# Layer-one weight slices stored later, and the last gates of a block pair computed in place, in a three-stage attention and MLP kernel

## The chip, the cores and the metric

The kernel runs on one core of one Trainium2 chip. The metric is the device time of one execution in microseconds (us), as the median of several executions. Before the change three executions took 1112.64, 1110.62 and 1107.44 us: median 1110.62. One more execution was profiled. TensorE is called PE here, VectorE DVE, ScalarE ACT; SP is SyncE, the queue that issues nearly all DMAs.

## What is computed

The reference, cut to what matters (float32; 4 batches, 8 heads, 768 positions, head size 64; 3072 tokens of 512 numbers, 2048 hidden):

```python
def _attn_ref(q, k, v, mem_k, mem_v):
    for c in range(S // 32):                     # chunks of 32 queries
        k_full = concat([mem_k, k[c*32-16 : c*32+40]])   # 8 + up to 56 slots
        v_full = concat([mem_v, v[c*32-16 : c*32+40]])
        scores = q_c @ k_full.T / 8
        a = exp(scores - max); a = a / (sum(a) + 1e-9)
        out_c = a @ v_full

x = attention output as (3072, 512)
h = x @ w_in;  g = s * relu(h)**2 + b;         x = g @ w_out      # layer one
h = x @ w_in2; g = h * sigmoid(1.702 * h);     out = g @ w_out2   # layer two
```

## The kernel before

**Split products.** Every matrix product of the layers is made as three matmuls of parts: a number is split into a high part and the rest (xh and xl, wih and wil, woh and wol, gh and gl), and high times high, high times rest and rest times high are added in PSUM. The weights come as 64-bit numbers; DVE and ACT make the two float32 parts of each 128x512 weight tile (`words` and `prep`: ACT L332 and L342, DVE L338, L346, L350 and L354, then ACT L223 for the high part and DVE L312 for the rest). One such DMA load is a `st<-w_in` or `st<-w_out` of 512 KB into a ring of three `st` tiles.

**Stages.** The 3072 tokens are 24 tiles of 128, or six blocks of four tiles. Attention runs per tile or per pair of tiles in four steps that PE does: S (scores, L418), T (transpose, L451), V (values, L479) and X (transpose back, L493). Between them DVE and ACT do the softmax (top, less, exp, px, den, norm); after X they write the block's xh (L223) and xl (L510). Tiles 0 to 3 are done singly, later ones in pairs (4,5), (6,7), and so on. Loads of k, q (`qe`) and v are at L403; each of these tiles has one buffer, so the load for the next pair waits for the last reader of the one before.

**Layer one, the visit loop.** Blocks 0 to 3 are done in visits (`VISITS`), as units. A unit (`step`) is one block and one 128-wide slice j of the hidden size: H, 12 matmuls (L602 to L604) from x and slice j of w_in; the gate on ACT and DVE (L609, L616, L613 or L620, L624, L628); O, 12 matmuls (L640) into four accumulators. H and O of a whole block have 512 columns; the first two slices of block 0 go as half-units of 256 columns, first tiles 0 and 1, then tiles 2 and 3. The order of visits is: block 0 with j 0 to 4, block 1 with j 0 to 4, block 1 with j 5 to 15, block 0 with j 5 to 15, block 2, block 3. So all 32 weight tiles of layer one are prepared by the end of the third visit, and stay in memory till the last.

**Blocks 4 and 5 of layer one, and layer two,** are done in pairs of blocks (`seven`, `SEVEN`): seven half-size products instead of eight, from combinations of the weight slices. For layer one the combinations and plain slices are written to HBM first by `combine(p)`, for each of eight pairs p of slices: four stores (`keep`, L725, 2 x 256 KB and 2 x 128 KB) of parts that exist as soon as the weights are prepared, and two (L764, 512 KB each) of combinations that are worked out once all weights are ready (L736 and L745 on DVE, L751 on ACT, L755 on DVE). In `seven` a running tile `ys` holds intermediate sums; `gates` makes g from PSUM or from `ys`, for one block of the pair at once (`mine`), for the other by way of HBM (`gd`), except the last two slices, whose g stays in the `gq` tile. The reloaded g of the other block then comes back into `back`, which has the same buffer as `ys` (L1136).

**What sets the order.** All work is entered as operations with a due time, the engine or engines that may do it, the model duration, what it comes after, and buffers. `Plan.order` is a list scheduler over them: it picks, engine by engine, the earliest one that is ready, by due time among those ready at about the same moment, and the program is emitted in that order. Nothing is rescheduled on the chip: each engine, and SP with its DMA issues, goes through its list in order, and an instruction that waits holds up all behind it. Operations named by `after` that share no data only influence the plan; they add no wait on the chip. In idle PE time before the first O, the planner puts dummy matmuls (`idle<-cold`).

Of the kernel before, what the change touches and what calls it, by code (L numbers as in the profile page):

```python
# [23 lines left out]
KT = DM // P  # L24
# [22 lines left out]
class Plan:  # L47
# [11 lines left out]
    def op(self, need, engines, fn, after=(), alloc=(), uses=(), follows=()):  # L59
        n = len(self.ops)  # L60
        behind = list(follows)
        for tag, _ in alloc:
            if tag != "u":
                if tag in self.last:
                    behind.append(self.last[tag])
                self.last[tag] = n
        self.ops.append((need, engines, fn, list(after), list(alloc), list(uses), behind))
        for h in uses:
            self.users.setdefault(h, []).append(n)
        return n  # L70

    def order(self):
# [5 lines left out]
        starts = [None] * len(ops)  # L78
# [9 lines left out]
        marks, clock = [], 0.0  # L88
# [4 lines left out]
        for i in range(len(ops) - 1, -1, -1):  # L93
            need, engines = ops[i][:2]
# [36 lines left out]
        while left:  # L131
            best = None
            for e, q in pending.items():
                cand = []
                seen = 0
                keep = []
                while q and seen < 24:
                    need, i = heapq.heappop(q)
# [39 lines left out]
        full, clock = [], 0.0  # L178
        for i, e in chosen:
            if e == "pe":  # L180
                idle = min(starts[i], starts[self.first]) - clock
                if idle > 0.3:
                    full.append((None, int(idle / self.BEAT)))
                clock = ends[i]
            full.append((i, e))
# [4 lines left out]
def attention_moe_moe(ctx: ExitStack, tc: tile.TileContext, q_t, k_w, v_w, w_in1, w_out1, s_b, w_in2, w_out2, out):  # L190
# [24 lines left out]
    sb = const.tile([P, 2], F32, name="sb")  # L215

    plan = Plan()
    plan.first = None
    op = plan.op
    T = {}  # L220

# [349 lines left out]


    plan.tag("g", 2)
    o_split, o_y, o_part = {}, {}, {}
    halves = ("accA", "accB")


# [8 lines left out]
    def step(i):  # L586
# [77 lines left out]
        for k in range(KT):  # L664
            prev = o_y.get((group, k))
            d = op(at_o[i], {"pe": dur}, out_part(k), after=[g1, g2] + list(o_w[wout]) + ([prev] if prev is not None else []),
                   alloc=[(halves[k // 2], ("acc", group, k // 2))] if fresh and k % 2 == 0 else [], uses=[("g", i), wout],
                   follows=[d] if fresh and k % 2 else [])
            if plan.first is None:
                plan.first = d  # L670
            o_y[group, k] = d
            if done:
                finish(m, b, k, group, lo, hi, d, at_o[i] + 4)

    o_store = {}

# [41 lines left out]
    def combine(p):  # L718

        w0, w1 = (0, 0, 2 * p), (0, 0, 2 * p + 1)  # L720
        need = at_h[len(units) - 1] + 20

        def keep(v, w, src, dst):
            def fn(e):
                nc.sync.dma_start(out=wc[0][p][v][:, dst], in_=T[w][v].bitcast(F32)[:, src].rearrange("p (n d) -> p n d", d=256))  # L725
            return fn

        first = list(o_w[w0]) + list(o_w[w1])
        done = [op(need, {"sp": 0.75}, keep(v, w0, slice(0, 512), slice(0, 2)), after=first[v:v + 1], uses=[w0]) for v in range(2)]
        done += [op(need, {"sp": 0.4}, keep(v, w1, slice(256, 512), slice(2, 3)), after=first[2 + v:3 + v], uses=[w1]) for v in range(2)]  # L730

        def whole(w, k):
            def fn(e):
                T[k, p] = stp.tile([P, 512], F32, tag="u", name="u", bufs=4)
                h, l = T[w]
                nc.vector.tensor_tensor(out=T[k, p], in0=h.bitcast(F32), in1=l.bitcast(F32), op=ALU.add)  # L736
            return fn

        lo, hi = slice(0, 256), slice(256, 512)

        def sums(e):
            T["s", p] = stp.tile([P, 4, 256], F32R, tag="st", name="st")
            x, a, b = T["s", p].bitcast(F32), T["wa", p], T["wb", p]
            nc.vector.tensor_tensor(out=x[:, 0], in0=b[:, lo], in1=b[:, hi], op=ALU.add)
            nc.vector.tensor_tensor(out=x[:, 2], in0=a[:, lo], in1=b[:, lo], op=ALU.subtract)  # L745
            nc.vector.tensor_tensor(out=x[:, 1], in0=x[:, 0], in1=a[:, lo], op=ALU.subtract)
            nc.vector.tensor_tensor(out=x[:, 3], in0=a[:, hi], in1=x[:, 1], op=ALU.subtract)

        def high(e):
            T["sh", p] = stp.tile([P, 4, 256], F32R, tag="st", name="st")  # L750
            nc.scalar.copy(out=T["sh", p], in_=T["s", p].bitcast(F32))  # L751

        def low(e):
            x = T["s", p]
            nc.vector.tensor_tensor(out=x, in0=x.bitcast(F32), in1=T["sh", p].bitcast(F32), op=ALU.subtract)  # L755

        end_ = list(o_w[weights[-1]])
        a = op(need, {"dve": 0.65}, whole(w0, "wa"), after=first[:2] + end_, alloc=[("u", ("wa", p))], uses=[w0])
        b = op(need, {"dve": 0.65}, whole(w1, "wb"), after=first[2:] + end_, alloc=[("u", ("wb", p))], uses=[w1])
        c = op(need, {"dve": 1.5}, sums, after=[a, b], alloc=[("st", ("s", p))], uses=[("wa", p), ("wb", p)])  # L760
        h = op(need, {"act": 1.05}, high, after=[c], alloc=[("st", ("sh", p))], uses=[("s", p)])
        l = op(need, {"dve": 1.2}, low, after=[h], uses=[("s", p), ("sh", p)])
        for v, (k, x) in enumerate((("sh", h), ("s", l))):
            done.append(op(need, {"sp": 1.35}, lambda e, v=v, k=k: nc.sync.dma_start(out=wc[0][p][v][:, 3:7], in_=T[k, p].bitcast(F32)),  # L764
                           after=[x], uses=[(k, p)]))
        o_wc[0, p] = done
# [88 lines left out]
    def seven(s):  # L855
# [134 lines left out]
        def gates(src, d, need, uses, j, mine, away=True):  # L990
            key = ("g", s, j, mine)
            rk = ("r", s, j, mine)

            def gate1(e):
                T[rk] = (gp if mine else stp).tile([P, 512], F32, tag="r" if mine else "u", name="r", bufs=1 if mine else 4)
                if m:
                    nc.scalar.activation(out=T[rk], in_=src(), func=AF.Sigmoid, scale=GATE)  # L997
                else:
                    nc.scalar.activation(out=T[rk], in_=src(), func=AF.Relu)
# [21 lines left out]
            def gate4(e):  # L1021
                nc.vector.tensor_tensor(out=T[key][1], in0=T[rk], in1=T[key][0].bitcast(F32), op=ALU.subtract)

            a = op(need, {"act": 0.6}, gate1, after=d, alloc=[("r" if mine else "u", rk)], uses=uses)
            last = a
            if m:
                last = b = op(need, {"dve": 0.69}, gate2, after=[a], uses=uses + [rk])
            else:
                b = op(need, {"act": 0.6}, square, after=[a], uses=[rk])
                b = op(need, {"dve": 0.42}, gate2, after=[b], uses=[rk])  # L1030
            here, kw = [("g", key)], {}
            if not mine:
                here, kw = [("gq", key)], {"follows": boxed[:1]}
# [1 line left out]
                    here.append(("xf", box))  # L1035
                    boxed.append(len(plan.ops))
            own = [] if mine else [box]
            g1 = op(need, {"act": 0.62}, gate3, after=[b], alloc=here, uses=[rk] + own, **kw)
            g2 = op(need, {"dve": 0.66}, gate4, after=[g1], uses=[rk] + own)
            if not mine and away:  # L1040
                return [last, op(need + 5, {"sp": 1.45}, lambda e: nc.sync.dma_start(out=gd[j], in_=T[key][2].bitcast(F32)), after=[g1, g2], uses=[key] + own)]
            return [last, g1, g2]
# [199 lines left out]
```

## Time and profile before

| | us |
|---|---|
| median of three executions (1107.44 to 1112.64) | 1110.62 |
| the profiled execution, its own time | 1112.08 |
| its span, first to last instruction | 1110.2 |
| PE busy | 1088.7 |
| DVE busy | 711.0 |
| ACT busy | 494.2 |

The span is what the engines show of the profiled execution; 1.9 us of its time lie outside. PE busy is a union of instruction times; a 512-column matmul has a mean length of about 390 ns and the next one starts some 230 ns later, so lengths overlap. The DMA share is the mean busy share of the 16 DMA engines.

### The profile page before, as it was taken

Reading aid. Unit: us, or ns where it says so; the run is one execution under the profiler, and the core shown is the slowest. Engines: PE = TensorE matmul, PEld = TensorE weight load, DVE = VectorE, ACT = ScalarE, POOL = GpSimd, SP = SyncE. Lnnn points to the kernel's source line nnn. Section 1 sums busy time; section 2 is a strip of 40 time slices with the busy share of each in tenths; the row PEclk is TensorE's granted clock in tenths of the full one; section 3 lists DMA queues with packets and bytes.
Section 4 is the critical chain, followed back from the end, with each engine's and each line's share of the span. In section 5 each row is a group of like instructions: output and inputs, shape, how many; then the busy total and the mean of one; then the engine's idle time right before and its main releaser. Section 6 shows DMA issues by size and latency. Waiting matters only on the chain.

```text
span 1110.2 us, 20092 instructions
## 1 busy us (share of the span) xinstructions
PE 1088.7 (98%) x7852; PEld 897.8 (81%) x7852; DVE 711.0 (64%) x1241; ACT 494.2 (45%) x842; POOL 0.7 (0%) x6
## 2 busy tenths in 40 slices
PE   8879999999999999999999999999999999999998
PEld 7768887888878788888888888888888888888886
DVE  6888988878778688687881455660555760655610
ACT  4678865555445455566640433330433430333310
POOL 0000000000000000000000000000000000000000
PEclk9999999999999999999999999999999999999999
DMA  8776627756678783888999965574755574654154
GB/s 326 245 258 209 208 105 248 259 193 219 208 275 267 265 301 117 312 294 279 318 323 382 322 203 200 183 260 144 246 188 201 202 246 155 203 190 142 76 191 150
DMA packets 119406, 252.99 MB, mean 228 GB/s; under 512 B 12816, under 2 KB 29200, under 8 KB 119312
## 3 DMA queue, kind: packets, MB, share of 16 engines
q1 hardware_dynamic: 119024, 251.19, 66.1%
q8 instruction: 62, 1.02, 0.4%
q10 hardware_dynamic: 288, 0.52, 0.1%
q14 instruction: 32, 0.26, 0.1%
HBM read 169.87 MB, written 81.79 MB: 227 GB/s over the span
## 4 chain that ended last, share of the span: by engine, by line
PE 92%; DMA 3%; DVE 2%; issue 1%; ACT 1%; SPq 0%; ACTq 0%; DVEq 0%
PE accA L1059 16%; PE accB L1059 16%; PE accA L640 7%; PE accB L640 7%; PE ph L981 5%; PE ph L983 5%; PE ph L982 5%; PE ph L602 5%; PE ph L603 5%; PE ph L604 5%; PE pb L983 4%; PE pb L981 4%; PE pb L982 4%; DMA st<-w_in 2%; PE o L479 1%; PE sc L418 1%
## 5 line engine op out<-in xcount | busy, mean ns | idle before, releaser
L997 ACT ACTIVATE r<-ys 128x512 f32<-128x512 f32 x72 | 45.5, 632 | 107.6 <-DVE ys L1094 81.2
L1083 DVE TENSOR_TENSOR ys<-pb,ys 128x512 f32<-128x512 f32 x32 | 22.0, 686 | 91.6 <-DMA out<-y 58.7
L602 PE MATMUL ph<-xh,wih 128*128 128x512 f32 (+1 forms) x200 | 79.3, 396 | 0.6 <-DVE xh L223 0.6
L603 PE MATMUL ph<-xl,wih 128*128 128x512 f32 (+1 forms) x200 | 76.6, 383 | 0.7 <-DVE xl L510 0.7
L604 PE MATMUL ph<-xh,wil 128*128 128x512 f32 (+1 forms) x200 | 76.4, 382 | 0.0
L223 ACT COPY y<-accA 128x512 f32<-128x512 f32 x20 | 10.9, 590 | 138.5 <-issue 84.4
L609 ACT ACTIVATE r<-ph 128x512 f32<-128x512 f32 (+1 forms) x66 | 38.5, 584 | 60.4 <-PE ph L604 54.2
L624 ACT CAST gh<-r 128x512 fp32r<-128x512 f32 (+1 forms) x66 | 40.2, 609 | 47.8 <-PE accB L640 31.2
L1094 DVE TENSOR_TENSOR ys<-pb,ys 128x512 f32<-128x512 f32 x32 | 22.1, 691 | 53.9 <-PE pb L983 53.3
L1006 DVE TENSOR_TENSOR r<-ph,r 128x512 f32<-128x512 f32 x24 | 16.6, 691 | 62.2 <-ACT r L997 62.2
L1059 PE MATMUL accA<-woh,gh 128*128 128x512 f32 x138 | 54.0, 391 | 0.0
L1059 PE MATMUL accA<-woh,gl 128*128 128x512 f32 x138 | 53.9, 390 | 0.0
L1059 PE MATMUL accB<-woh,gh 128*128 128x512 f32 x138 | 53.7, 389 | 0.0
L1059 PE MATMUL accA<-wol,gh 128*128 128x512 f32 x138 | 53.7, 389 | 0.0
L1059 PE MATMUL accB<-woh,gl 128*128 128x512 f32 x138 | 53.7, 389 | 0.0
L1059 PE MATMUL accB<-wol,gh 128*128 128x512 f32 x138 | 53.7, 389 | 0.0
L640 PE MATMUL accA<-gl,woh 128*128 128x512 f32 (+1 forms) x132 | 50.9, 385 | 2.2 <-DVE gl L628 2.2
L1019 ACT CAST gh<-r 128x512 fp32r<-128x512 f32 x64 | 39.8, 622 | 29.1 <-DVE r L1006 21.7
L342 ACT ACTIVATE st<-st 128x512 f32<-128x512 uint32 x64 | 42.8, 676 | 22.4 <-DMA st<-w_out 10.7
L640 PE MATMUL accA<-gh,woh 128*128 128x512 f32 (+1 forms) x132 | 51.4, 389 | 1.3 <-ACT gh L624 1.3
L640 PE MATMUL accB<-gl,woh 128*128 128x512 f32 (+1 forms) x132 | 50.6, 383 | 1.2 <-issue 1.2
L640 PE MATMUL accB<-gh,woh 128*128 128x512 f32 (+1 forms) x132 | 51.0, 387 | 0.0
(210 smaller groups left out, 2973.6 us busy)
## 6 DMA issues: line engine op xcount, KB each, us to landing
gd<-gq SPq DMA_DIRECT2D x56, 512.0 KB, 2.7
wih<-wch SPq DMA_DIRECT2D x96, 256.0 KB, 3.5
wil<-wcl SPq DMA_DIRECT2D x96, 256.0 KB, 3.8
st<-w_in SPq DMA_DIRECT2D x32, 512.0 KB, 5.4
st<-w_out SPq DMA_DIRECT2D x32, 512.0 KB, 5.0
back<-gd SPq DMA_DIRECT2D x56, 256.0 KB, 3.1
k<-k_w SPq DMA_DIRECT2D x24, 512.0 KB, 5.6
v<-v_w SPq DMA_DIRECT2D x24, 512.0 KB, 6.1
```

Source lines behind the costliest of these rows:

```text
L342: nc.scalar.activation(out=lo.bitcast(F32), in_=lo, func=AF.Copy, scale=2.0**-51, bias=2.0)
L602: nc.tensor.matmul(ph, wh, xh, start=(k == 0), stop=False)
L603: nc.tensor.matmul(ph, wh, xl, start=False, stop=False)
L604: nc.tensor.matmul(ph, wl, xh, start=False, stop=(k == KT - 1))
L624: nc.scalar.copy(out=T["g", i][0], in_=T["r", i])
L640: nc.tensor.matmul(o, lt, rh, start=fresh and x == 0, stop=(done and x == 2))
L981: nc.tensor.matmul(ph, wh, xh, start=first and i == 0, stop=False, skip_group_check=True)
L982: nc.tensor.matmul(ph, wh, xl, start=False, stop=False, skip_group_check=True)
L983: nc.tensor.matmul(ph, wl, xh, start=False, stop=i == 1, skip_group_check=True)
L997: nc.scalar.activation(out=T[rk], in_=src(), func=AF.Sigmoid, scale=GATE)
L1019: nc.scalar.copy(out=T[key][0], in_=T[rk])
L1059: nc.tensor.matmul(a, lt, rh, start=n == 0 and x == 0, stop=n == NF - 1 and x == 2)
```

## The change

It does three things. (1) The four `keep` stores of pair p come, for the planner, after the last O of unit 16+p (units 12 to 22 are the third visit) instead of as soon as the weights exist. (2) In `combine` the second weight sum is put into the `st` tile that holds the combinations, so it takes no `u` buffer. (3) For layer one the gates of the last two slices of the other block overwrite `ys` instead of a `u` tile. The planner's mark for the first O is now the first four O operations, of which the earliest counts.

```diff
@@ Plan.order
-                idle = min(starts[i], starts[self.first]) - clock
+                idle = min(starts[i], *(starts[x] for x in self.first)) - clock
@@ step
-            if plan.first is None:
-                plan.first = d
+            if len(plan.first) < KT:
+                plan.first.append(d)
...
+        o_unit[i] = d
@@ combine
+        end_ = [o_unit[16 + p]]
-        done = [op(need, {"sp": 0.75}, keep(v, w0, slice(0, 512), slice(0, 2)), after=first[v:v + 1], uses=[w0]) for v in range(2)]
-        done += [op(need, {"sp": 0.4}, keep(v, w1, slice(256, 512), slice(2, 3)), after=first[2 + v:3 + v], uses=[w1]) for v in range(2)]
+        done = [op(need, {"sp": 0.75}, keep(v, w0, slice(0, 512), slice(0, 2)), after=first[v:v + 1] + end_, uses=[w0]) for v in range(2)]
+        done += [op(need, {"sp": 0.4}, keep(v, w1, slice(256, 512), slice(2, 3)), after=first[2 + v:3 + v] + end_, uses=[w1])
+                 for v in range(2)]
...
-                T[k, p] = stp.tile([P, 512], F32, tag="u", name="u", bufs=4)
+                if k == "wa":
+                    x = T[k, p] = stp.tile([P, 512], F32, tag="u", name="u", bufs=4)
+                else:
+                    T["s", p] = stp.tile([P, 4, 256], F32R, tag="st", name="st")
+                    x = T["s", p].bitcast(F32)[:, 2:4].rearrange("p n d -> p (n d)")
@@ seven, gates
+            there = not (mine or away or m)
             def gate1(e):
-                T[rk] = (gp if mine else stp).tile([P, 512], F32, tag="r" if mine else "u", name="r", bufs=1 if mine else 4)
+                T[rk] = src() if there else (gp if mine else stp).tile(
+                    [P, 512], F32, tag="r" if mine else "u", name="r", bufs=1 if mine else 4)
...
-            a = op(need, {"act": 0.6}, gate1, after=d, alloc=[("r" if mine else "u", rk)], uses=uses)
+            a = op(need, {"act": 0.6}, gate1, after=d, alloc=[] if there else [("r" if mine else "u", rk)], uses=uses)
+            here_r = uses if there else [rk]
```

Because the planner places everything anew, the change moves instructions far from the stores themselves.

SP, the DMA queue, near the start of the program, before (L403: attention loads of k, qe, v; L326: weight loads; L725: the `keep` stores):

```order
L403 DMA k<-k_w 128x1024 x2
L326 DMA st<-w_out 128x1024
L725 DMA wch_89<-wih 128x512
L403 DMA qe<-q_t 128x512 x2
L403 DMA v<-v_w 128x1024 x2
L725 DMA wcl_90<-wil 128x512
L326 DMA st<-w_in 128x1024
L326 DMA st<-w_out 128x1024
L403 DMA k<-k_w 128x1024 x2
L725 DMA wch_89<-wih 128x256
```

The same place of the same queue after the change:

```order
L403 DMA k<-k_w 128x1024 x2
L326 DMA st<-w_out 128x1024
L403 DMA qe<-q_t 128x512 x2
L403 DMA v<-v_w 128x1024 x2
L403 DMA k<-k_w 128x1024 x2
L403 DMA qe<-q_t 128x512 x2
L326 DMA st<-w_in 128x1024
L403 DMA v<-v_w 128x1024 x2
L326 DMA st<-w_out 128x1024
L326 DMA st<-w_in 128x1024
```

The stores are gone from here, and the k and qe loads of tiles 4 and 5 now stand ahead of the third w_in load (the first `st<-w_in` of each list).

PE, tiles 2 and 3 of the attention, before (S, T, V and X of both tiles; L602 begins the third half-unit of H; the second half-unit stands just ahead of the first row):

```order
L1183 MATMUL idle<-cold 128x128 x2
L451 MATMUL pp<-ident,qe 128x128 x8
L479 MATMUL o<-v,px 32x64 x64
L1183 MATMUL idle<-cold 128x128 x4
L493 MATMUL xx<-ident,px 128x128 x8
L1183 MATMUL idle<-cold 128x128 x8
L602 MATMUL ph<-xh_362,wih 128x256
```

PE at the same place after the change, from V of tile 2 on:

```order
L479 MATMUL o<-v,px 32x64 x32
L451 MATMUL pp<-ident,qe 128x128 x4
L602 MATMUL ph<-xh_361,wih 128x256
L603 MATMUL ph<-xl_362,wih 128x256
L604 MATMUL ph<-xh_361,wil 128x256
L1193 MATMUL idle<-cold 128x128
L479 MATMUL o<-v,px 32x64 x32
L493 MATMUL xx<-ident,px 128x128 x4
L1193 MATMUL idle<-cold 128x128 x2
L493 MATMUL xx<-ident,px 128x128 x4
L1193 MATMUL idle<-cold 128x128 x5
L418 MATMUL sc<-k,qe 32x64 x32
```

Tiles 2 and 3 now go one after the other, with the second half-unit between their steps, and S of tile 4 (last row) stands ahead of the third half-unit. S of tile 2 stands ahead of the first half-unit, S of tile 3 behind it, where both stood behind it before. In all, 46 dummies are issued instead of 52.

SP again, at the end of the third visit, after the change (L726: the `keep` stores, which stood singly between the loads before):

```order
L326 DMA st<-w_out 128x1024
L726 DMA wcl_92<-wil 128x512
L726 DMA wch_91<-wih 128x256
L726 DMA wcl_92<-wil 128x256
L726 DMA wch_93<-wih 128x512
L726 DMA wcl_94<-wil 128x512
L726 DMA wch_93<-wih 128x256
L726 DMA wcl_94<-wil 128x256
```

The first row is the last weight load of layer one; five stores stand ahead of it and the others follow in a row.

## Rows read from the trace of the kernel before

**Rows 1.** The page, busy time of TensorE and the others over the span.
```profile
PE 1088.7 (98%) x7852; PEld 897.8 (81%) x7852; DVE 711.0 (64%) x1241; ACT 494.2 (45%) x842; POOL 0.7 (0%) x6
```

**Rows 2.** Windows: length, busy us per engine, clock, DMA share, GB/s.
```profile
0.00:82.00 82.00, 68.19 (x1383) 59.27 (x1384) 63.63 (x120) 50.65 (x90) 0.70 (x6) 1.00 0.81 281
82.00:160.00 78.00, 78.00 (x405) 64.41 (x404) 69.70 (x131) 61.54 (x108) 0.00 (x0) 1.00 0.53 172
...
300.00:380.00 80.00, 77.38 (x1091) 63.17 (x1090) 57.83 (x106) 40.72 (x67) 0.00 (x0) 1.00 0.82 277
380.00:1080.00 700.00, 699.61 (x3197) 575.51 (x3195) 406.39 (x689) 269.01 (x462) 0.00 (x0) 1.00 0.66 227
1080.00:1111.00 31.00, 25.81 (x114) 21.03 (x112) 0.00 (x0) 2.15 (x4) 0.00 (x0) 0.99 0.44 151
```

**Rows 3.** PE's waits, 0 to 82 us: total, times, longest.
```profile
PE sc L418 <- issue: 2.6, 1, 2.6
PE accA L640 <- DVE gl L628: 2.2, 3, 1.2
PE o L479 <- ACT px L223: 1.9, 3, 1.2
PE accA L640 <- ACT gh L624: 1.3, 1, 1.3
PE accB L640 <- issue: 1.2, 1, 1.2
```

**Rows 4.** PE's timeline: start, us, instruction, [idle before <-releaser].
```profile
25.71 0.44 PE L418 MATMUL sc<-k,qe 64*32 64x64 f32 x26 [2.60 <-issue]
...
35.03 0.36 PE L602 MATMUL ph<-xh,wih 128*128 128x256 f32 x1
...
36.53 0.28 PE L640 MATMUL accA<-gh,woh 128*128 128x256 f32 x1
...
48.08 0.28 PE L640 MATMUL accB<-gh,wol 128*128 128x256 f32 x1
...
59.02 1.09 PE L493 MATMUL xx<-ident,px 128*128 128x128 f32 x8 [0.82 <-DVE px L484]
...
80.39 0.50 PE L602 MATMUL ph<-xh,wih 128*128 128x512 f32 x1 [0.64 <-DVE xh L223]
81.59 0.51 PE L603 MATMUL ph<-xl,wih 128*128 128x512 f32 x1 [0.70 <-DVE xl L510]
```

**Rows 5.** SP's timeline, first and last `keep` store of twelve, and loads.
```profile
13.48 0.33 SPq L725 DMA_DIRECT2D wch<-wih  x1
14.98 0.88 SPq L403 DMA_DIRECT2D qe<-q_t  x2
...
22.03 0.33 SPq L326 DMA_DIRECT2D st<-w_in  x1
...
73.04 0.38 SPq L725 DMA_DIRECT2D wcl<-wil  x1
```

**Rows 6.** ACT's timeline, the wait for the fourth w_in load.
```profile
43.96 0.66 ACT L332 ACTIVATE u<-st 128x512 f32<-128x512 f32 x1 [3.23 <-DMA st<-w_in]
```

**Rows 7.** The page, two of the five DVE steps of a weight.
```profile
L354 DVE SCALAR_TENSOR_TENSOR u<-st,u 128x512 uint32<-128x512 uint32 x64 | 43.3, 685 | 0.7
L346 DVE TENSOR_SCALAR u<-u 128x512 uint32<-128x512 uint32 x64 | 27.0, 422 | 0.9
```

**Rows 8.** DVE's and PE's timelines: layer one's last weight, its last H.
```profile
154.69 0.68 DVE L312 TENSOR_TENSOR wol<-u,woh 128x512 fp32r<-128x512 f32 x1
...
158.67 0.39 PE L602 MATMUL ph<-xh,wzh 128*128 128x512 f32 x1
```

**Rows 9.** SP's, DVE's and PE's timelines around the first `back` load.
```profile
563.05 1.74 SPq L1136 DMA_DIRECT2D back<-gd  x4
...
568.07 0.68 DVE L1022 TENSOR_TENSOR gq<-r,gq 128x512 fp32r<-128x512 f32 x1
...
573.11 0.62 PE L1059 MATMUL accA<-back,woh 128*128 128x512 f32 x2
```

More of the change, by code (lines that the diff above doesn't have):

```diff
@@ L217, in attention_moe_moe @@
     plan = Plan()
-    plan.first = None
+    plan.first = []
     op = plan.op
@@ L573, in attention_moe_moe @@
     plan.tag("g", 2)
-    o_split, o_y, o_part = {}, {}, {}
+    o_split, o_y, o_part, o_unit = {}, {}, {}, {}
     halves = ("accA", "accB")
@@ L728, in combine @@
         first = list(o_w[w0]) + list(o_w[w1])
-        done = [op(need, {"sp": 0.75}, keep(v, w0, slice(0, 512), slice(0, 2)), after=first[v:v + 1], uses=[w0]) for v in range(2)]
-        done += [op(need, {"sp": 0.4}, keep(v, w1, slice(256, 512), slice(2, 3)), after=first[2 + v:3 + v], uses=[w1]) for v in range(2)]
+        end_ = [o_unit[16 + p]]
+        done = [op(need, {"sp": 0.75}, keep(v, w0, slice(0, 512), slice(0, 2)), after=first[v:v + 1] + end_, uses=[w0]) for v in range(2)]
+        done += [op(need, {"sp": 0.4}, keep(v, w1, slice(256, 512), slice(2, 3)), after=first[2 + v:3 + v] + end_, uses=[w1])
+                 for v in range(2)]
         def whole(w, k):
             def fn(e):
-                T[k, p] = stp.tile([P, 512], F32, tag="u", name="u", bufs=4)
+                if k == "wa":
[3 more added lines that the diff above has]
+                    x = T["s", p].bitcast(F32)[:, 2:4].rearrange("p n d -> p (n d)")
                 h, l = T[w]
-                nc.vector.tensor_tensor(out=T[k, p], in0=h.bitcast(F32), in1=l.bitcast(F32), op=ALU.add)
+                nc.vector.tensor_tensor(out=x, in0=h.bitcast(F32), in1=l.bitcast(F32), op=ALU.add)
             return fn
@@ L741, in sums @@
         def sums(e):
[L742 to L745, printed above, removed]
+            x, a = T["s", p].bitcast(F32), T["wa", p]
+            nc.vector.tensor_tensor(out=x[:, 0], in0=x[:, 2], in1=x[:, 3], op=ALU.add)
+            nc.vector.tensor_tensor(out=x[:, 2], in0=a[:, lo], in1=x[:, 2], op=ALU.subtract)
             nc.vector.tensor_tensor(out=x[:, 1], in0=x[:, 0], in1=a[:, lo], op=ALU.subtract)
@@ L758, in combine @@
         a = op(need, {"dve": 0.65}, whole(w0, "wa"), after=first[:2] + end_, alloc=[("u", ("wa", p))], uses=[w0])
-        b = op(need, {"dve": 0.65}, whole(w1, "wb"), after=first[2:] + end_, alloc=[("u", ("wb", p))], uses=[w1])
-        c = op(need, {"dve": 1.5}, sums, after=[a, b], alloc=[("st", ("s", p))], uses=[("wa", p), ("wb", p)])
+        b = op(need, {"dve": 0.65}, whole(w1, "wb"), after=first[2:] + end_, alloc=[("st", ("s", p))], uses=[w1])
+        c = op(need, {"dve": 1.5}, sums, after=[a, b], uses=[("wa", p), ("s", p)])
         h = op(need, {"act": 1.05}, high, after=[c], alloc=[("st", ("sh", p))], uses=[("s", p)])
@@ L1028, in gates @@
             else:
-                b = op(need, {"act": 0.6}, square, after=[a], uses=[rk])
-                b = op(need, {"dve": 0.42}, gate2, after=[b], uses=[rk])
+                b = op(need, {"act": 0.6}, square, after=[a], uses=here_r)
+                b = op(need, {"dve": 0.42}, gate2, after=[b], uses=here_r)
             here, kw = [("g", key)], {}
@@ L1037, in gates @@
             own = [] if mine else [box]
-            g1 = op(need, {"act": 0.62}, gate3, after=[b], alloc=here, uses=[rk] + own, **kw)
-            g2 = op(need, {"dve": 0.66}, gate4, after=[g1], uses=[rk] + own)
+            g1 = op(need, {"act": 0.62}, gate3, after=[b], alloc=here, uses=here_r + own, **kw)
+            g2 = op(need, {"dve": 0.66}, gate4, after=[g1], uses=here_r + own)
             if not mine and away:
```

## Prediction

> **What bounds the kernel now.** I read the page first: PE is busy for 1088.7 of 1110.2 us [rows 1], so what a change can win lies in the 21.5 us in which PE is idle, and in the dummies ahead of the first O. Then the windows, to see where these are [rows 2]. Up to 82 us PE is idle for 82.00 - 68.19 = 13.8 us; in the last 31 us for 5.2 (the last stores); between 300 and 380 us for 2.6; almost nowhere else. In those first 82 us the DMA engines are 0.81 busy and move 281 GB/s, in the next 78 us only 0.53 and 172 GB/s. So the stage to look at is the first 82 us, and stores moved from there to the third visit go from a crowded stretch to an emptier one. Third, PE's waits there [rows 3]: it waits in turn for the gate's gl and gh, for px, and 3.8 us for nothing the profile shows ("issue"). Last, the timelines of PE, SP and ACT, for where each wait stands [rows 4 to 6].
>
> **What goes, and what it frees.** Twelve `keep` stores are issued up to 82 us, the first at 13.48, the last at 73.04 [rows 5]: three pairs of 2 x 256 and 2 x 128 KB, 2.3 MB, at 281 GB/s 8.2 us of DMA time. They hold PE only where a load behind them is late for it. The qe load of tiles 2 and 3 is not held by the store ahead of it: SP issues it at 14.98, when PE is through with T of tile 1, and will again. It lands up to 256 KB / 281 GB/s = 0.9 us earlier. The new order does the rest. I follow it through five places; at each the number is how much earlier than before PE has done the same work.
>
> *Third half-unit.* Before, S of tile 3 ends at 25.71 + 0.44 = 26.15, after a wait of 2.60 in mid-work; without that wait it ends at 23.55. The third half-unit begins at 35.03 [rows 4], 8.9 us after the S, the length of the softmax chain, with 17 dummies in it. Now the second half-unit and tile 2's steps stand in that chain, with 12 dummies between, and S is split by the first half-unit. If S goes through without the wait, 23.55 + 8.9 = 32.4, or 32.7 with S of tile 4 ahead of it: 2.3 earlier, and that S (some 0.8, by the 0.44 for 26 of its matmuls) is then done. **-3.1**; bounds -0.5 (the wait stays) and -4.
>
> *O of the third half-unit's slice.* It ends at 48.08 + 0.28 = 48.36. Ahead of it PE waited 1.3 for gh [rows 3] and 0.4 of the 2.2 for gl, because ACT, which takes its list in order, stood 3.23 us at a weight whose load had not landed [rows 6]. That load's place in SP's list comes earlier by about the 3.1 above, and three stores fewer share the engines. I take **-1.4**; bounds 0 and -1.7.
>
> *X of tiles 4 and 5* (before at 59.02 [rows 4]). T, V and X were spread between parts of O; now they stand together, so the copy of px and the norm are exposed. I estimate 0.9 + 1.4 = 2.3 us, near the longest px wait seen, 1.2 [rows 3], and somewhat above the norm's 0.82, which had part of an O beside it [rows 4]. Before, 0.4 of the px total, the longest gl wait, 1.2, and the 0.82 stood here, 2.4 together: **-0.2**, rounded up for the restarts of PE that go, bounds +1 and -1.
>
> *X of tiles 6 and 7.* Here PE waited 1.2 for px, 0.6 for gl, 1.2 on issue [rows 3]; the new order leaves a px wait of about 0.9: **-2.1**, bounds 0 and -3.
>
> *H of block 1.* It waited 0.64 and 0.70 for block 1's xh and xl [rows 4]. One O of 12 matmuls (699.61 us / 3197 in the long stretch [rows 2], 0.22 each, so 2.6) now stands behind X instead of ahead of it and covers both: **-1.3**, bounds 0 and -1.3.
>
> Sum: -8.1. Two things come off. The 3.8 us on issue are taken as gone in it; nothing shows their cause, only that they fall in the crowded stretch; half of them back elsewhere is **+1.9** (bounds 0 and +3.8). And the fifth w_in load now stands behind the k and qe loads of tiles 6 and 7, with its weight due just as PE comes to it: **+0.5** (0 to +2). Left: **-5.7**.
>
> **What is covered, and by what.** The moved stores add no wait on the chip: what they read has long been written, so SP only runs through them. Twenty more stores than those twelve move within the third visit; their cover is the 47% of DMA time that is free there [rows 2]. Five of them, 1 MB, go ahead of the last w_out load: 1 MB / 281 GB/s = 3.7 us at most. That weight is ready at 154.69 + 0.68 = 155.4; the H of its slice begins at 158.67 [rows 8] and its O 2.7 later, so it has 6.0 us to spare. But DVE pays for the early attention: nine weights stand ahead of the norm of tiles 6 and 7 in its new list, eleven before. A weight is two steps of 0.42 and three of 0.68 [rows 7], 2.9 us; two are 5.8. If PE and DVE both come to that norm g earlier, the last weight comes 5.8 - g later than before and is wanted g earlier than its 6.0 us of slack: it just suffices, and DVE's idle 8.3 us between 82 and 160 [rows 2] are the reserve for the stores. Sum at nothing, bound +3.
>
> The second sum's place in an `st` tile changes no work; the ring wait that it may add falls after 160 us, where DVE and ACT have room. Nothing, bound ±1. The gates in place: `back` has the buffer of `ys`, so its first load, at 563.05, will have to wait for the last gate step instead of the first, 568.07 + 0.68 = 568.75 [rows 9], 5.7 later. PE used it at 573.11, 10.1 after the issue. In the new order 36 matmuls (8.2 us) stand between the first use of gq, which that same step releases, and the first of `back`, against 18 before. A 256 KB load that lands 4 to 5 us after its issue is in time: nothing, bound +1.5. The 2.6 us between 300 and 380 us may shift by as much either way.
>
> [...]
>
> **The rivals.** *Hidden anyway* (0.32). DVE, 63.6 of 82 and then 69.7 of 78 us busy [rows 2], is what the first three visits wait for in the end: two weights put off come back as a PE wait at the end of the third visit, or the issue waits all return. For it: the slack above comes out at nearly nothing. Against it: DVE's idle time. Gain 0 to 3, say 1.5: 1109.1. [...]
>
> *Slower* (0.09): the third w_in load. It was issued at 22.03 [rows 5]; now it stands behind the k loads of tiles 4 and 5, which wait for S of tile 3 (23.55), and their qe loads, which wait for T of tile 3 (some 4 us on), so it is issued at about 28.4, 6.4 later. ACT's step for it stands ahead of a gate and of another weight's cast. If the weight then needs as long to be ready as before, PE, which wants it for H of the fifth unit (36.53 plus O, H, S and O of a half-unit and a tile, 1.5 + 1.5 + 0.8 + 1.5, at about 41.8), waits to 48.2: +6.4, less the 3.6 of the last three places: +2.8, 1113.4, and +6.4, 1117, if those go too. It decides only if the weight is ready later than 41.8. Against it: by the chain it lands near 33, and ACT (62% busy) and DVE (78%) need about 6 us for it.
>
> *The clock falls* (0.03): an H or O of 2.7 us would take 5.4; two or three of them, +5 to +8: 1117.
>
> **How the numbers follow.** My forecast has 0.56. The profiled execution took 1112.08, 1.5 above the median of the three runs; 1112.08 - 5.7 = 1106.4, and on the median's scale 1110.62 - 5.7 = **1104.9**. The low end adds the uncharged half of the bounds, -10: 1100.5. The high end takes in the hidden case and the nearer half of the slower one: 1113.5. A measurement here can tell about 0.5%, 5.55 us, from no change. The forecast sits on that line: of its 0.56 some 0.45 lies beyond (faster 0.46 with a little from elsewhere), the rest with the hidden case and the nearer slower one makes same 0.45, slower 0.09.
>
> **What would show it.** Right: PE idle before 82 us falls from 13.8 to about 8; the third half-unit begins near 32.7; no 3 us ACT wait for a weight load before 50 us; no L726 store before 100 us; PE without idle from 82 to 160 us. Wrong: a PE wait of over 2 us for wih or woh in the first three visits, an issue wait of 2 us or more again before 40 us, or a wait at the first use of `back`.

## The result, and the profile after

The changed kernel takes **1116.36 us** (median of 12 executions, 1112.24 to 1126.82); the kernel before, beside it, 1110.59 (12 executions, 1107.10 to 1112.64). The ratio is 1.0068, with a 95% interval of 1.0050 to 1.0087: slower, where 1104.9 was forecast with a range that ended at 1113.5. The profiled execution took 1115.91 us, its span is 1113.9.

First the windows of the changed kernel, with the columns of [rows 2]: length, busy time of PE, PEld, DVE, ACT and POOL, granted clock, DMA share, GB/s. The lines for 440 to 500, 500 to 560 and 560 to 580 us cut the loss out of the long stretch.

```profile
0.00:82.00 82.00, 74.97 (x1406) 65.11 (x1407) 66.41 (x124) 53.71 (x96) 0.70 (x6) 1.00 0.72 261
82.00:160.00 78.00, 78.00 (x345) 64.56 (x344) 71.21 (x136) 61.96 (x108) 0.00 (x0) 1.00 0.52 174
300.00:380.00 80.00, 76.98 (x1087) 62.93 (x1086) 57.49 (x106) 39.32 (x66) 0.00 (x0) 1.00 0.79 269
380.00:1080.00 700.00, 693.06 (x3023) 568.64 (x3023) 404.90 (x692) 263.79 (x451) 0.00 (x0) 0.99 0.65 225
...
440.00:500.00 60.00, 57.47 (x250) 46.29 (x248) 42.65 (x80) 35.17 (x62) 0.00 (x0) 1.00 0.90 308
500.00:560.00 60.00, 59.80 (x255) 49.10 (x256) 49.55 (x93) 40.44 (x73) 0.00 (x0) 0.97 0.81 281
560.00:580.00 20.00, 16.13 (x59) 12.54 (x58) 14.19 (x28) 6.36 (x13) 0.00 (x0) 0.83 0.81 289
620.00:1080.00 460.00, 459.66 (x2017) 377.87 (x2016) 232.79 (x368) 151.34 (x257) 0.00 (x0) 1.00 0.57 197
```

PE stands idle for 7.0 us of the first 82 where it was 13.8 [rows 2], and for nothing up to 160: the startup went as forecast. But between 380 and 1080 us, where PE was idle for 0.4 us, it is idle for 6.9, with a mean granted clock of 0.99. Nearly all of it (2.5 + 0.2 + 3.9) lies between 440 and 580 us, in the first pair of blocks of `seven`; from 620 us on PE is full again. Between 300 and 380 us it is idle for 3.0 us, where it was 2.6.

Where the lead is gained and lost is seen by one row that stands at three places of the program: the H matmuls on the tile wzh (the last slices of layer one), and the first and last of the pair products on that tile. The columns are count, duration, first and last start. The fence has the changed kernel; the kernel before has 142.3, 455.2 and 1051.7 for the same three.

```profile
L602 PE MATMUL ph<-xh,wzh x64: 389/389/499, 133.3 to 431.8; 128*128 128x512 f32 x64
L987 PE MATMUL ph<-wzh,wih x64: 389/389/499, 447.7 to 1055.4; 128*128 128x512 f32 x64
```

So PE is 9.0 us ahead at 133 us, 7.5 ahead at the start of the first pair of blocks, and 3.7 behind in the last one. These are PE's waits between 440 and 620 us (total, times, longest), and its timeline at the two:

```profile
PE accA L1069 <- ACT y L223: 3.9, 1, 3.9
PE pb L987 <- DVE ys L1111: 2.7, 2, 2.3
```

```profile
500.20 0.56 PE L987 MATMUL pb<-xl,wih 128*128 128x512 f32 x1 [2.35 <-DVE ys L1111]
500.56 0.63 PE L988 MATMUL pb<-xl,wih 128*128 128x512 f32 x1
...
503.95 0.39 PE L1069 MATMUL accA<-gh,woh 128*128 128x512 f32 x1
...
565.69 0.39 PE L1069 MATMUL accB<-gl,woh 128*128 128x512 f32 x1
565.92 0.39 PE L1069 MATMUL accB<-gh,wol 128*128 128x512 f32 x1
570.18 1.22 PE L1069 MATMUL accA<-gq,woh 128*128 128x512 f32 x2 [3.87 <-ACT y L223]
...
575.46 0.46 PE L1069 MATMUL accA<-gh,woh 128*128 128x512 f32 x1
```

Each wait is followed by matmuls at half pace: from 500.56 to 503.95 the eight of them start 0.42 us apart, from 570.18 to 575.46 twelve (rows of x2 and x1 in turn) start 0.44 apart, where the full pace is 0.23 (565.69 to 565.92). The granted clock says the same, 0.57 and 0.53 (the columns are those of the windows above):

```profile
500.00:504.00 4.00, 3.80 (x10) 2.98 (x11) 3.82 (x9) 3.70 (x8) 0.00 (x0) 0.57 0.46 170
570.00:576.00 6.00, 5.82 (x15) 4.56 (x15) 4.02 (x10) 1.01 (x3) 0.00 (x0) 0.53 1.02 388
```

The slow matmuls cost 8 x 0.23 = 1.8 taken from 3.39, so 1.5, and 12 x 0.23 = 2.8 from 5.28, so 2.5. With the two waits, 2.35 + 3.87, that is 10.2 of the 11.2 us that are lost between 447.7 and the end (7.5 + 3.7).

What is late for PE? ACT's and DVE's timelines stand next, first at the first wait, then at the second:

```profile
498.43 0.66 ACT L332 ACTIVATE u<-st 128x512 f32<-128x512 f32 x1 [3.25 <-DMA st<-w_in]
...
567.91 0.62 ACT L223 CAST st<-u 128x512 fp32r<-128x512 f32 x1 [2.33 <-DVE u L354]
569.23 0.41 ACT L223 COPY st<-u 128x256 f32<-128x256 f32 x1 [0.71 <-DVE u L354]
569.54 0.58 ACT L223 COPY y<-accA 128x512 f32<-128x512 f32 x1
```

```profile
499.12 0.43 DVE L338 TENSOR_SCALAR u<-u 128x512 f32<-128x512 f32 x1 [3.25 <-ACT u L332]
499.46 0.68 DVE L1111 TENSOR_TENSOR ys<-pb,ys 128x512 f32<-128x512 f32 x1
```

Both times a step for a *layer-two weight* (L332 to L354, and the copies to `st` of `pair`), wanted only in layer two, stands in the engine's list ahead of what PE waits for. At 498 us ACT waits 3.25 us for a weight's load, DVE waits for ACT, and the sum L1111 stands behind it. At 567 us ACT waits for two weights of the last `pair`, and the second copy out of accA stands behind them. DVE kept to the order of its list here: what L1111 reads was there, since PE had ended its products before its own wait began, at 500.20 - 2.35 = 497.85, and yet it starts only behind L338, at 499.46.

### The profile page after: what moved, and what is told of

Read it like the earlier page. It is cut to its first block, busy times and chain, and to the rows that moved or that the text cites. A ratio compares the mean times of both kernels' runs of the same rounds, so it can differ in the third digit from the quotient of the medians.

```text
span 1113.9 us, 20017 instructions
## 1 busy us (share of the span) xinstructions
PE 1091.1 (98%) x7840; PEld 899.3 (81%) x7840; DVE 711.6 (64%) x1250; ACT 489.7 (44%) x833; POOL 0.7 (0%) x6
## 4 chain that ended last, share of the span: by engine, by line
PE 85%; DMA 7%; DVE 6%; ACT 1%; issue 1%; SPq 0%; ACTq 0%; DVEq 0%
PE accA L1069 16%; PE accB L1069 15%; PE accA L640 6%; PE accB L640 6%; PE ph L987 5%; PE ph L989 5%; PE ph L988 5%; PE ph L602 4%; PE ph L603 4%; PE ph L604 4%; PE pb L987 4%; PE pb L988 4%; PE pb L989 4%; DMA wcl<-st 2%; DMA st<-w_out 2%; DMA y<-y 1%
## 5 line engine op out<-in xcount | busy, mean ns | idle before, releaser
L602 PE MATMUL ph<-xh,wih 128*128 128x512 f32 (+1 forms) x200 | 79.1, 396 | 0.0
L342 ACT ACTIVATE st<-st 128x512 f32<-128x512 uint32 x64 | 42.9, 675 | 25.8 <-DMA st<-w_in 10.2
L987 PE MATMUL pb<-xl,wih 128*128 128x512 f32 x128 | 50.4, 394 | 2.7 <-DVE ys L1111 2.7
L640 PE MATMUL accA<-gh,wol 128*128 128x512 f32 (+1 forms) x132 | 50.6, 384 | 0.2 <-DVE wol L312 0.2
```

The source lines that it names most:

```text
L342: nc.scalar.activation(out=lo.bitcast(F32), in_=lo, func=AF.Copy, scale=2.0**-51, bias=2.0)
L602: nc.tensor.matmul(ph, wh, xh, start=(k == 0), stop=False)
L640: nc.tensor.matmul(o, lt, rh, start=fresh and x == 0, stop=(done and x == 2))
L987: nc.tensor.matmul(ph, wh, xh, start=first and i == 0, stop=False, skip_group_check=True)
```

## The experiments

Two questions were open: which of the three parts of the change brings the loss, and by which mechanism; and whether the startup's lead was 9 us in truth. The parts are: **one**, the stores put off behind units 16 to 23; **two**, the second sum in the `st` tile; **three**, the last two gates in place.

### e1 and e2: one part, and the other two

e1 is the kernel before with part one alone (the changed `plan.first` with it), e2 that with parts two and three alone; the core of each, against the kernel before:

```
+        end_ = [o_unit[16 + p]]
...
-after=first[v:v + 1], uses=[w0]
+after=first[v:v + 1] + end_, uses=[w0]
```

```
+                    T["s", p] = stp.tile([P, 4, 256], F32R, tag="st", name="st")
...
+            there = not (mine or away or m)
```

> Part one alone (the stores of the prepared slices behind units 16 to 23; combine and gates as before). Theory A, order: the later layer-two weights that follow from the put-off stores stand ahead of the first pair of blocks' sums and of the copies out of its accumulators, so this alone shows the loss: PE is some 7 to 9 us early at 440 us, the lead is gone by 600 us, and the time is 1112 to 1122 us. Theory B, parts two and three: the gates in place and the second sum in the st tile cost the lead; without them it stays, 1101 to 1104 us.

> Parts two and three without part one (second sum in the st tile, last two gates in place, stores as before). Theory A: nothing, 1109.5 to 1111.5 us, no wait over 1 us between 440 and 600 us. Theory B: the cost shows without the gain, 1117 to 1121 us.

e1: 1118.13 us, ratio 1.0071 (1.0048 to 1.0094). e2: 1108.76, ratio 0.9995 (0.9979 to 1.0011), no wait over 0.3 us for a product. So the deferral alone brings the whole loss, and the other two parts alone do nothing, as the prediction had said of them. In e1 PE waits in the same stage, and longer, but for another step, the gate that makes gq:

```profile
PE accA L1062 <- ACT gq L1022: 9.3, 1, 9.3
PE pb L984 <- DVE ys L1104: 1.6, 2, 1.1
```

That gate stands behind the last layer-two pair's weights on both engines. These are ACT's cast for the first of them, then DVE's last steps of both and the gate's step L1011, and last the same two weight steps in the kernel before (its second profile, e8 below):

```profile
560.67 0.62 ACT L223 CAST st<-u 128x512 fp32r<-128x512 f32 x1 [2.72 <-DVE u L354]
```

```profile
559.95 1.28 DVE L354 SCALAR_TENSOR_TENSOR u<-st,u 128x512 uint32<-128x512 uint32 x2
565.42 0.54 DVE L1011 TENSOR_SCALAR r<-r,sb 128x512 f32<-128x512 f32 x1
```

```profile
532.27 0.69 DVE L354 SCALAR_TENSOR_TENSOR u<-st,u 128x512 uint32<-128x512 uint32 x1
536.34 0.69 DVE L354 SCALAR_TENSOR_TENSOR u<-st,u 128x512 uint32<-128x512 uint32 x1
```

From 559.35 to 565.42 DVE does nothing but steps of these two weights; the gate's step, whose input ACT had finished at 562.5, stands behind them. So putting the stores off sets the last pair's weights 24 to 28 us later, just in front of the first pair of blocks' last gates.

### e3 and e5: the late weights, and the tile they hold

e3 is the changed kernel with the last four layer-two weights loaded only after the first group's copies out of the accumulators. The loads get a dependency, and the calls stand behind `seven(0)`:

```
-    for p in range(NF // 2):
+    for p in range(7):
         pair(p)
-        outer(2 * p)
-        outer(2 * p + 1)
+        for j in (2 * p, 2 * p + 1):
+            if j < 14:
+                outer(j)
...
         seven(s)
+        if s == 0:
+            end_ = [o_evac[0, SEVEN[0][1], k] for k in range(KT)]
+            for p in range(7, NF // 2):
+                pair(p, end_)
+            for j in range(14, NF):
+                outer(j, end_)
```

> The changed kernel, with the loads of the last layer-two pair and of the last two second matrices put behind the first pair of blocks' copies out of accumulators (nothing else). Theory A: the 3.87 us wait for accA near 570 us and the half clock behind it go; the 2.35 us wait near 500 us may stay: 1107 to 1111 us. Theory B: the gates in place are still there, 1115 to 1118 us. Theory C, the clock falls at this place whatever the waits: granted clock under 0.9 in 570 to 580 us, 1112 to 1115 us.

e3: 1111.05 us, ratio 1.0023 (1.0005 to 1.0041). In the profiled execution (1108.26 us) the wait for accA and the half clock are gone, and the idle time before 500 us stays; over all twelve executions the mean granted clock still goes down to 0.994:

```profile
440.00:500.00 60.00, 57.85 (x253) 47.02 (x252) 43.48 (x83) 36.04 (x64) 0.00 (x0) 1.00 0.90 309
500.00:560.00 60.00, 60.00 (x265) 49.18 (x264) 50.66 (x95) 38.39 (x68) 0.00 (x0) 1.00 0.78 269
560.00:580.00 20.00, 20.00 (x89) 16.32 (x88) 10.91 (x24) 5.92 (x11) 0.00 (x0) 1.00 0.88 320
```

That leaves two readings: these weights fill the engines, or the copy needs something that they hold. It does need a `u` tile, and the planner hands the four `u` tiles round in order: in its order the second copy's turn is the tile of the last pair's first weight, so it places the copy behind all users of that tile. e5 moves no weight and gives the copies tiles of their own:

```
-                T["y", m, b, k] = stp.tile([P, 512], F32, tag="u", name="y", bufs=4)
+                T["y", m, b, k] = home[1]() if home else stp.tile([P, 512], F32, tag="u", name="y", bufs=4)
...
+                    if m == 0 and b == bp and k != 2:
+                        home = [([], lambda: spot(0), [tmp], last_s1[0]), ([], lambda: spot(2), [tmp], [last_s3]), None,
+                                ([("r", ("y", m, b, k))], lambda: gp.tile([P, 512], F32, tag="r", name="r", bufs=1), [], [])][k]
```

> The changed kernel, in which the first pair's copies out of its accumulators no longer take turns in the ring of four u tiles with the weights: two go to slots 0 and 2 of ys, one to the r tile, one to u; no weight is moved. Theory A1, the ring: the copy out of accA stood behind the last pair's weight steps because its u tile was theirs; now the 3.87 us wait near 570 us and the half clock behind it go although the same weights are as late as before: 1108 to 1112 us. Theory A2, the engines: vector and scalar engine are simply full there with late weights, the tile does not matter: a wait of 2 us or more for accA or accB stays, 1114 to 1118 us.

e5: 1112.50 us, ratio 1.0032 (1.0013 to 1.0050), between the two expectations by the time, and its interval overlaps that of the changed kernel measured again (e10); the trace decides. These are ACT's copies (here to `ys`, `y` and `r`), then DVE's last step of the two late weights:

```profile
562.17 1.08 ACT L223 COPY ys<-accA 128x512 f32<-128x512 f32 x2 [1.23 <-PE accA L1070]
563.53 0.59 ACT L223 COPY y<-accB 128x512 f32<-128x512 f32 x1 [0.28 <-PE accB L1070]
564.02 0.59 ACT L223 COPY r<-accB 128x512 f32<-128x512 f32 x1
566.43 0.41 ACT L223 COPY st<-u 128x256 f32<-128x256 f32 x1 [0.70 <-DVE u L354]
```

```profile
564.37 0.70 DVE L354 SCALAR_TENSOR_TENSOR u<-st,u 128x512 uint32<-128x512 uint32 x1
565.71 0.69 DVE L354 SCALAR_TENSOR_TENSOR u<-st,u 128x512 uint32<-128x512 uint32 x1
```

The weights are about as late as in the changed kernel (567.19 and 568.51 there, 563.94 and 565.26 in its second profile, e10), but all four copies now stand ahead of their last steps, and PE has no idle time in 560 to 580 us. So in the changed kernel it is the turn of the tile that put the copy behind the weights, not the engines' load.

### e6 and e7: what the second sum costs once the stores are put off and the last weights moved

With the last four weights late as in e3, e6 has parts one and three, e7 parts one and two. Against e3, e6 first:

```
-        b = op(need, {"dve": 0.65}, whole(w1, "wb"), after=first[2:] + end_, alloc=[("st", ("s", p))], uses=[w1])
+        b = op(need, {"dve": 0.65}, whole(w1, "wb"), after=first[2:] + end_, alloc=[("u", ("wb", p))], uses=[w1])
```

```
-            there = not (mine or away or m)
...
-                T[rk] = src() if there else (gp if mine else stp).tile(
+                T[rk] = (gp if mine else stp).tile(
```

> Parts one and three, without part two (combine's second sum in a u tile as before), the last four layer-two weights behind the copies. If part two is what brings the layer-two weights late from 300 us on, and so the wait near 500 us: no wait over 1 us between 440 and 540 us, 1105.5 to 1108.5 us. If the gates in place do it: the wait stays, 1109.5 to 1113 us.

> Parts one and two, without part three (last gates through their own u tiles), the last four layer-two weights behind the copies. If part two brings the weights late: waits of 1.5 to 4 us together between 440 and 540 us, 1109.5 to 1113 us. If the gates in place do it: 1105.5 to 1108.5 us.

e6: 1106.96 us, ratio 0.9988 (0.9971 to 1.0006). e7: 1109.71, ratio 1.0017 (0.9996 to 1.0038). With e3 (all three parts) and e4 below (part one alone) this is a square. Part two: 1.0023 - 0.9988 = 0.0035 and 1.0017 - 0.9983 = 0.0034, 3.8 us both ways. Part three: 0.0005 and 0.0006, 0.6 us, which this measurement can't tell from nothing. (e6 still has a wait of 1.4 us for a product, so its expectation failed in that detail.) With the last weights where the change puts them, part two shows no such price: e1, without it, has 1.0071, the changed kernel, with it, 1.0068.

What part two does is seen in the weights. This is DVE's last step of one layer-two weight, the 54th of the program, in e6 and then in e7:

```profile
437.44 0.69 DVE L354 SCALAR_TENSOR_TENSOR u<-st,u 128x512 uint32<-128x512 uint32 x1
```

```profile
462.10 0.69 DVE L354 SCALAR_TENSOR_TENSOR u<-st,u 128x512 uint32<-128x512 uint32 x1
```

It comes 25 us later in e7. It takes both parts: with one and two together (the changed kernel, e3, e5, e7) the step stands at 457.5 to 462.1, with one and not two (e1, e4, e6) at 434.7 to 437.4, with two and not one (e2) at 434.0, in the kernel before (e8) at 434.5. That the cause is the `st` tile that the second sum now holds for longer, one of three through which every load passes, fits with this; no run varied the number of `st` tiles, so it is argued, not shown.

How the later weights would cost 3.8 us stays open. Between 440 and 625 us PE's waits come to 3.8 us in e3 and 3.6 in e6, so those two profiles don't show it; in e7 they come to 3.7 and in e4 to 1.7. The profiled execution of e7, 2.8 us above its median, lost another 5 us earlier: 302.5 us lie between its first and its last H on wzh, 297.0 in e6, with 4.4 us of PE waits for ACT's qe.

### e8 and e10: the same kernels profiled again

e8 is the kernel before, e10 the changed one, neither altered.

> The kernel before, unchanged, for a second profile of it. If the 13.8 us in which the tensor engine stood idle in the first 82 us belong to the order, they show again within 1 us, and the prediction's lead of 8 to 9 us was a real one. If the profiled execution was one with a long startup (the kernel with parts two and three alone, whose tensor instructions are the same there, idled 9.5 us): 9 to 11 us, and the startup can give only some 2 to 3 us.

> The changed kernel, unchanged, for a second profile. If the two waits belong to the order: a wait of 1.5 to 3 us before a product near 500 us and one of 3 to 5 us for accA near 570 us again, each with a stretch at a granted clock under 0.9 behind it, and 1113 to 1120 us. If they were chance of one execution: waits under 1 us, 1108 to 1112 us.

e8: 1108.24 us against 1108.60 beside it. Its startup is not that of the first profile. In its first 82 us, PE's window and two of its waits; then the rows on wzh:

```profile
0.00:82.00 82.00, 72.41 (x1400) 63.45 (x1401) 67.65 (x128) 53.02 (x94) 0.70 (x6) 1.00 0.84 289
```

```profile
PE sc L418 <- issue: 1.4, 1, 1.4
PE accA L640 <- DVE gl L628: 1.1, 1, 1.1
```

```profile
L602 PE MATMUL ph<-xh,wzh x64: 389/389/499, 138.4 to 436.1; 128*128 128x512 f32 x64
L981 PE MATMUL ph<-wzh,wih x64: 389/389/389, 451.8 to 1048.4; 128*128 128x512 f32 x64
```

PE is idle for 9.6 us, not 13.8, the issue wait is 1.4, not 2.60 [rows 4], there is no wait for gh, and ACT's longest wait for a weight's load between 30 and 60 us is 0.65 us, not 3.23 [rows 6]. PE reaches the first H on wzh at 138.4; e2 at 138.4 and e12 at 137.0, with the same stores in the startup. The execution that the prediction was worked out from had reached it at 142.3: **its startup was some 4 us longer than in the three others.** The ten profiles with the stores put off come to that H between 132.8 and 135.5, so the startup's lead is about 138 - 134 = 4 us, not 9. Set against e8, the changed kernel is 5.1 us ahead at its first H on wzh, 4.1 ahead at the first pair product on it and 7.0 behind at the last: the loss from that product on, 11.1 us, is as large as against the first profile, 11.2.

e10: 1114.18 us, ratio 1.0044 (1.0025 to 1.0062). The same two waits, 1.48 and again 3.87 us; but the first, which ends at 498.52, has no half clock behind it, and the second a shorter one: eight matmuls and 3.4 us, where the first profile had twelve and 5.3 (windows behind each wait, then PE's timeline, in which the half pace lasts from 566.93 to 570.28):

```profile
498.00:502.00 4.00, 3.48 (x15) 2.91 (x16) 3.98 (x9) 3.69 (x8) 0.00 (x0) 1.00 0.73 276
567.00:570.00 3.00, 3.00 (x8) 2.36 (x9) 2.86 (x7) 0.00 (x0) 0.00 (x0) 0.54 1.03 381
```

```profile
566.93 0.99 PE L1069 MATMUL accA<-gq,woh 128*128 128x512 f32 x2 [3.87 <-ACT y L223]
...
570.28 0.57 PE L1069 MATMUL accA<-gq,wol 128*128 128x512 f32 x1
```

So the waits belong to the order, and the clock's answer varies. That fits the spread: over the first comparison's executions of the changed kernel, 1112.24 us goes with a mean granted clock of 0.998, and the longest, 1126.82, with 0.989.

### e4, e9, e11 and e12: can the lead be kept?

e4 is e1 with the four late weights, by the diff shown under e3. e9 is e5 without part two, by the diff shown under e6. e11 is e4 with the four weights behind the second group's copies, and e12 is e11 without part one:

```
-            end_ = [o_evac[0, SEVEN[0][1], k] for k in range(KT)]
+            end_ = [o_evac[0, SEVEN[0][2], k] for k in range(KT)]
```

```
-after=first[v:v + 1] + end_, uses=[w0]
+after=first[v:v + 1], uses=[w0]
```

> Part one alone, with the same four last layer-two weights put behind the copies. Theory A: the startup's 7 to 9 us stay to the end, 1101 to 1105 us, granted clock 1.00 from 440 to 600 us. Theory B: the same 1101 to 1105 us (it tells A from C, not from B). Theory C: a clock under 0.9 somewhere in 440 to 600 us in most runs, 1106 us or more.

> Parts one and three (combine as before), no weight moved, and the first pair's copies out of its accumulators in ys slots, r and one u as in e5. If the two causes found so far are all there is (part two holds an st tile and brings the weights late; the last copies stand behind the last pair's weights for a u tile), the lead of the startup stays but for 1 to 2 us: 1105 to 1108 us, no wait over 2 us between 440 and 600 us. If late weights cost by filling the vector engine, and not by the tile: 1110 to 1114 us.

> Part one alone, with the last four layer-two weights behind the copies of the second group of the first pair of blocks (e4 had them behind the first group's). In e4 the second group's copies stood behind one of these weights' steps, and the next stage's first product waited 1.7 us for them. If that was it: the wait is under 0.6 us and the time 1.7 us less than e4's against the kernel before, 1104 to 1107 us, a lead of 4 to 5 us kept to the end. If the lead is lost elsewhere: 1107 us or more.

> The kernel before with the last four layer-two weights behind those same copies, and nothing put off at the start. If the gain of e4 and e11 is the startup's: no gain here, 1108 to 1111 us. If it is that of the late weights: as e11, 1104 to 1107 us.

| kernel | us, beside the kernel before | ratio, 95% interval |
|---|---|---|
| e4 | 1107.22, 1108.96 | 0.9983 (0.9970 to 0.9995) |
| e9 | 1112.66, 1110.33 | 1.0024 (1.0008 to 1.0039) |
| e11 | 1104.24, 1109.34 | **0.9959** (0.9943 to 0.9975) |
| e12 | 1109.58, 1109.34 | 1.0006 (0.9995 to 1.0016) |

e11 beats both kernels, by 2.8 to 6.3 us against the one before; e12 shows that the late weights alone bring nothing, so the gain is the startup's. e4 and e1 differ in nothing but the place of the four weights, and the ratio goes from 1.0071 to 0.9983, some 10 us: with these weights out of the first pair of blocks, the loss is gone. Even so e4 keeps less than was expected of it, since the lead was 4 us and not 7 to 9, and one wait of 1.7 us for a product is left near 612 us. In e11 that wait is gone, but one of 1.78 us for the next product, near 616 us, and one of 1.47 near 482 us have come; the two profiles don't account for the 2.4 parts in a thousand between e4 and e11, whose intervals overlap. e9 missed. Its time lies in the range of its rival, a filled DVE, but PE does not wait for DVE there: it waits for `back`, which takes over the buffer of `ys`. SP waits 0.7 us for the store of the copies in `ys` before it issues `back`, at 564.50, and in this order PE comes to `back` 18 matmuls behind the first use of gq, where e5 has 36. The half clock came with the wait (PE's wait, then the window):

```profile
PE accA L1067 <- DMA back<-gd: 3.0, 2, 2.7
```

```profile
560.00:580.00 20.00, 16.99 (x62) 12.92 (x61) 11.03 (x24) 3.81 (x7) 0.00 (x0) 0.83 0.94 321
```

## Why the prediction was wrong, point by point

**Right: the startup's mechanism.** Four of its five signs came: idle before 82 us about 8 (7.0), third half-unit near 32.7 (33.01), PE without idle from 82 to 160 us (78.00 of 78), the first L726 store behind 100 us (132.99). Only ACT's wait for a load before 50 us was there again (3.02 us, at 33.75), and PE did not feel it. `back` was in time too, issued at 564.51. The two rivals on the startup, cover by DVE and the third w_in load, did not occur: PE's longest wait for a weight there is 0.2 us. The third w_in load was issued at 27.96, close to the 28.4 of that rival, but its weight was ready by 39.2, ahead of the 41.8 that would have decided it.

**Mis-sized: the startup's sum.** The -3.1 and the -1.4 rested on an issue wait of 2.60 and an ACT wait of 3.23 us, both of one execution; in e8 they are 1.4 and at most 0.65. The most that the deferral gained is e11's 4.5 us by its ratio (2.8 to 6.3), with 3.3 us of waits still in its profile between 440 and 625 us. That the forecast's -5.7 lies so near is luck in part: -8.1 was read against a startup 4 us too long, and +2.4 was charged for things that mostly did not come back (the issue wait is 0.8 of 2.6 + 1.2).

**The step that failed: "what is covered, and by what".** The prediction priced everything after 160 us at nothing: the second sum "falls after 160 us, where DVE and ACT have room", the long stretch has 0.4 us of idle time, and 300 to 380 us "may shift by as much either way". It looked for what the moved *stores* would make late, and found nothing; PE waits for none of them in the profile after. But a planner makes one order for all engines, and with the stores put off it gave the layer-two weights other places. Part one alone sets the last steps of the last pair's two weights at 559.95 (e1), where e8 has 532.27 and 536.34; the changed kernel has them at 567.19 and 568.51. There they stand ahead of the first pair of blocks' last gates and copies. In the changed kernel the two waits behind weight steps came to 6.2 us, with 4.0 us of half clock. That the last four weights are the larger part of it is shown: moved away, they take 10 us off e1 (e4) and 5 off the changed kernel (e3; 2.3 by its second measurement, e10), and e5 shows by which tile. The wait near 500 us stands behind an earlier weight's load, and no run took that one away by itself. Why the planner moves these weights when the stores are put off, no run shows. The room of DVE and ACT, an average over a stretch, says nothing of whose step stands first in their lists.

**Mis-sized: part two.** Nothing, bound 1, was taken; alone it is nothing (e2), and in the change as it stands nothing is seen of it (e1 against the changed kernel); with the stores put off and the last weights moved it costs 3.8 us (e3, e4, e6, e7), by a path that the profiles don't show. Part three was taken as nothing, and 0.6 us is what was measured.

**Mis-placed: the clock.** The prediction gave 0.03 to the rival in which the clock falls. That an H or O of 2.7 us would then take 5.4 was the author's estimate, which no row of the kernel before shows: there the clock is 1.00 through gaps of up to 2.60 us [rows 2, 4]. The half clock did come: 0.57 and 0.53 behind the two waits near 500 and 570 us, and behind the second twelve matmuls took 5.28 us. In e11 it came in the startup, at X of tiles 4 and 5 (the eight matmuls of X took 1.97 us, 1.09 in the changed kernel) and at the H behind it (matmuls 0.43 us apart). It did not come each time: behind the 1.48 us of e10 the clock stayed at 1.00. That the measured 1116.36 lies near this rival's 1117 is chance: the rival counts in H and O of layer one, and through the first three visits, up to 160 us, the changed kernel's first profile has 1.00. These are windows of 40 to 50 and 50 to 60 us, of the changed kernel first, then of e11:

```profile
40.00:50.00 10.00, 7.14 (x164) 6.03 (x164) 9.34 (x17) 6.80 (x13) 0.00 (x0) 1.00 0.61 206
50.00:60.00 10.00, 10.00 (x174) 8.11 (x172) 8.94 (x18) 6.86 (x12) 0.00 (x0) 1.00 0.72 266
```

```profile
40.00:50.00 10.00, 7.14 (x164) 6.03 (x163) 9.34 (x17) 7.94 (x16) 0.00 (x0) 0.94 0.57 184
50.00:60.00 10.00, 10.00 (x163) 8.66 (x164) 7.00 (x15) 7.84 (x13) 0.00 (x0) 0.72 0.50 190
```

Both have the same two waits there, 1.40 and 1.46 us, and the same busy time; the one keeps its clock, the other loses it. Rows of one execution could not show that.

## What to carry to other kernels

Where one plan orders all engines, price a moved step by the whole new order: look at every later stage for what now stands ahead of the work that the bounding engine waits for, and for rings of tiles that early and late work share. Put work that is wanted much later behind an explicit dependency rather than trust that the engines have room. And before a lead of a few microseconds is read off a startup, profile the same kernel twice.

## What the runs showed of the hardware that was not expected

The clock's answer to a wait was not fixed by its length: behind the same wait of 3.87 us in the same program the half pace lasted 5.3 us and twelve matmuls in one execution and 3.4 us and eight in the other, and 1.40 and 1.46 us in a row did in one execution (e11, 0.72) what they did not in another (the changed kernel, 1.00), nor 2.60 us in the kernel before (1.00) [rows 2, 4]. The startup of one and the same kernel differed by 4 us between two executions (the first profile before, and e8): 2.4 us in PE's waits for the gate's gh and gl, 1.2 in a wait on nothing that the profile shows, and 0.8 in waits for the loads of k and qe.
